# Recurrent retention and a SiLU block on one core: three more units of k and q transposed by the DMA

## The chip, the core and the metric

The kernel runs on one core of a Trainium2 chip. Its engines are TensorE (PE: matrix products; its weight loads are shown apart as PEld), VectorE (DVE), ScalarE (ACT), GpSimd (POOL) and SyncE (SP), which here issues nearly all DMA transfers. The metric is the device time of one execution in microseconds; the number given for the kernel is the median of its runs. All matrix work is in 32-bit floats, split into parts so that products are exact enough.

## The reference

First a recurrent retention over 4 batches (b), 8 heads (h), 768 positions and 64 channels; then a two-layer block with SiLU on the result, with heads and channels side by side as 512 features:

```python
gamma = 1.0 - 2.0 ** (-5.0 - np.arange(H, dtype=np.float32))
for t in range(S):
    state = gamma[None, :, None, None] * state + np.einsum('bhd,bhe->bhde', k[:, :, t], v[:, :, t])
    y[:, :, t] = scale * np.einsum('bhd,bhde->bhe', q[:, :, t], state)
x = y.transpose(0, 2, 1, 3).reshape(B * S, H * D)
h = x @ w_in                      # 3072 x 512 by 512 x 2048
g = h * (1.0 / (1.0 + np.exp(-h)))
return g @ w_out                  # 3072 x 2048 by 2048 x 512
```

## The kernel before

**Units, visits, steps.** The 768 positions are cut into 6 chunks (c) of 128. A unit is one chunk of one batch, numbered 4c + b, so there are 24. Each unit goes through three stages in three successive visits. In visit m, unit m is staged (k and q are transposed, so that channels lie on partitions), unit m-1 gets its score and state products (L452, L462), and unit m-2 its output y (L501), which is split into three parts of x for the first layer. A step (c, f) is the first layer for one chunk and one of 16 slices f of 128 hidden features: eight products into the PSUM tile ha and four into hb (`multiply`, L650), then in `close_steps` a copy of ha by ScalarE (L660), a subtraction of hb by VectorE (L665), and the SiLU by ScalarE (L670). SP stores the result g to DRAM. After the 96 steps the second layer reads g back (L967).

**Order.** TensorE runs in the order of the program text. On the other engines, after the opening part, a planner orders the instructions by priority and by when it thinks their inputs are there; `queue(ins)` only says "not before `ins`". Things that are to follow a step's copy of ha are put into the list `behind_copy`, things that are to follow its subtraction into `behind_next`. The list `steps` fixes the order of steps: after (1,15) come (2,8) to (2,15), then (3,0), (3,1) and so on; (2,3) to (2,7) lie some twenty steps earlier. The list `at` says behind which step a visit stands: visit 14 behind (1,15), 15 behind (2,9), 16 behind (2,11), 17 behind (2,13), so that they are two steps apart; from visit 18 behind (3,1) on they are four steps apart.

**Two ways to transpose.** `stage_t` (L429 to L438) lets TensorE transpose k and q of a unit, four 128 x 128 transposes each into PSUM (L436), and ScalarE copy them out (L438). It is used for units below FAR = 17. From unit 17 on the DMA does it, in 16-bit planes: `part_t` (L407) lets GpSimd separate the high and low halves of the 32-bit words of q and of k (L412); `turn_t` (L416) lets SP issue one transposing DMA for each (L419); `join_t` (L422) lets ScalarE interleave the halves again (L426). For unit m these stand in visit m, one step later, and three steps later. `scale_k` (L382, L398) multiplies k by its decay factors, after the parting and two steps later; `scale_q` (L403) multiplies the joined q by gq, and `next_chunk` (L350) advances gq by a chunk, in four ScalarE instructions.

**Buffers.** Tiles of one tag share a number of buffers. k and the planes of q share "kf" (3), q and its turned planes "qf" (2), the planes of k and the transposed k "kt" (2), the turned k and the transposed q "qt" (3). The tag "wl" (1) holds the low part while a weight slice is split (L123 to L128). The y of chunk 2 are read back from DRAM by `late_y` (L583, batches 0 and 2 into "kt", 1 and 3 into "qt") and split by `late_x` (L557 to L563). g uses three buffers "hs". `load` (L145) issues the loads of k, q, v: in visit m for unit m+2, or m+1 where the unit is above FAR, and always m+1 for v. Between visits VectorE and ScalarE also turn the weights, which arrive as 64-bit words, into 32-bit floats (L196 to L217).

**The fence.** In each visit a GpSimd write of a token (L377) separates two groups of the products of y; a parting in a visit stands behind that fence on GpSimd.

Of the kernel before, what the change touches and what calls it, by code (L numbers as in the profile page):

```python
# [13 lines left out]
FP32 = mybir.dt.float32  # L14
# [19 lines left out]
def kernel(  # L34
# [31 lines left out]
    C = 128  # L66
# [72 lines left out]
    kqv = {"k": {}, "q": {}, "v": {}}  # L139
    EARLY = 2 * B  # L140

    FAR = 4 * B + 1
    early = {}

    def load(name, n):  # L145
        if n >= len(units):
            return
        c, b = units[n]
        src = {"k": k, "q": q, "v": v}[name]
        if n < EARLY:  # L150

            if n not in early:
                early[n] = wpool.tile([128, 3, H, D], FP32, tag=f"w{4 + n}", name=f"kqv_{n}")
            t = early[n][:, "kqv".index(name)]
        else:
            t = ld.tile([128, H, D], FP32, tag=f"{name}f", name=f"{name}f_{n}",
                        bufs=2 if name == "q" else 3)
        nc.sync.dma_start(out=t, in_=src[b, :, ds(c * C, C)].rearrange("h t d -> t h d"))
        kqv[name][n] = t
# [244 lines left out]

    planes, turned = {}, {}

    def part_t(n):  # L407

        for name, (p, tag, bufs) in (("q", (ld, "kf", 3)), ("k", (one, "kt", 2))):
            src = kqv[name].pop(n) if name == "q" else kqv[name][n]  # L410
            t = p.tile([128, 2 * H * D], U16, tag=tag, name=f"{name}p_{n}", bufs=bufs)
            nc.gpsimd.tensor_copy(out=t.rearrange("p (w h d) -> p w h d", w=2, h=H),  # L412
                                  in_=src.bitcast(U16).rearrange("p h (d w) -> p w h d", w=2))
            planes[name, n] = t

    def turn_t(n):  # L416
# [5 lines left out]
    def join_t(name, n):  # L422

        to, bufs = (qt, 3) if name == "q" else (kt, 2)
        to[n] = one.tile([128, HP, C], FP32, tag=f"{name}t", name=f"{name}t_{n}", bufs=bufs)
        nc.scalar.copy(out=to[n].bitcast(U16).rearrange("p a (t w) -> p w a t", w=2),  # L426
                       in_=turned.pop((name, n)).rearrange("p (w a) t -> p w a t", w=2))
# [153 lines left out]
    y_late = {}  # L581

    def late_y(b):  # L583
        tag = ("kt", "qt")[b % 2]
        y_late[b] = one.tile([128, KIN, C], FP32, tag=tag, name=f"yr_{b}", bufs=2 + b % 2)
        nc.sync.dma_start(out=y_late[b], in_=y_dram[b])

    def late_x(b):
# [9 lines left out]
    def halves(m):  # L598

        first, mid, last = (0 <= m - i < len(units) for i in range(3))  # L600
        if first and m < FAR:
            stage_t(m)
        if last:
            scores, states_with, yp = stage_y(m - 2)
            scores()
            states_with(0)
        yield
        if mid:
            sc, sums = score_tile(m - 1)
            stage_s(m - 1, sums)  # L610
            stage_a(m - 1, sc)
            if 1 < m <= 3 * B + 1 and units[m - 1][1] == 0:
                next_chunk()

            with queue(taken_out[0]) if m > 3 * B + 1 else ExitStack():
                finish_a(m - 1, sc, sums)
            scale_q(m - 1)
            if m > 3 * B + 1 and units[m - 1][1] == B - 1:

                behind_copy.append(next_chunk)  # L620
        if first and m < FAR:
            scale_k(m)
        if last:
            states_with(1)
            finish_y(m - 2, yp)

        if FAR <= m < len(units):
            with queue(fenced[0]):
                part_t(m)
        for name in "kqv":  # L630
            for n in (m + 1, m + 2):
                if n >= EARLY and n == (m + 1 if name == "v" or n > FAR else m + 2):
                    load(name, n)
        if EARLY + 2 <= m < 3 * B + 2:
            with queue(masked[0]):
                end_w()
                if m != 3 * B:
                    begin_w()


    pending = []

    def product_in(c, f):
# [264 lines left out]
    for i, x in enumerate(at):  # L908
# [4 lines left out]
    behind[1, NF - 1] = lambda: [late_x(3), visit(EARLY + 6)]  # L913


    far = {steps.index(x): EARLY + 6 + i for i, x in enumerate(at)
           if FAR <= EARLY + 6 + i < len(units)}
    for n, (c, f) in enumerate(steps):
        if n - 2 in far:
            behind_next.append(lambda m=far[n - 2]: scale_k(m))  # L920
        if n - 3 in far:
            behind_copy.append(lambda m=far[n - 3]: [join_t(name, m) for name in "qk"])
        product_in(c, f)
        put_g(1)
        store_w()
        if (c, f) in takes:
            take_w(taken_out[0], n < len(pairs + three))
        behind.get((c, f), lambda: None)()
        if n - 1 in far:
            turn_t(far[n - 1])  # L930
        if c == NC - 1:
            if f == 0:
                for i in range(W_READ):
                    get_w(i)
            if f < NF - 4:
                w_out(f)
            if f >= NF - 6:
                if f == NF - 6:
                    for n in range(G_AHEAD):
                        get(n)  # L940
                if f >= NF - S_AHEAD:
                    split(f - NF + S_AHEAD)
# [84 lines left out]
```

## Time and profile before

| | |
|---|---|
| time, median of 3 runs | 622.0 us (619.96 to 622.71) |
| the profiled execution: time, span | 619.42 us, 617.6 us |
| TensorE clock granted | full |
| span from 97 to 170 us | steps of chunks 0 to 2, visit 14 at the end |
| span from 170 to 204 us | visits 14 to 17, steps (2,8) to (2,15) |
| span from 204 to 303 us | chunks 3 and 4, visits 18 to 25 |
| span from 350 us | second layer |
| TensorE transposes (L436) | 68 for k, 68 for q; 272 and 273 ns each at the median, overlapping |
| planes parted (L412) | 7 for q, 7 for k; 1042 and 1051 ns |
| transposing DMAs (L419) | 7 and 7; issue 1304 and 1282 ns, landing after 4.1 and 3.6 us |
| ScalarE joins (L426) | 7 for q and 7 for k, about 1.36 us each |
| ScalarE evacuations of transposes (L438) | 0.58 us each |

A row of the page or of an answer of the trace gives the line of the kernel, the engine, the operation and the tiles that it writes and reads; "x4" is the number of instructions. In a list in order of time, the first number is the start in the span, the second the duration, and a bracket at the end says how long the engine was idle before and who released it.

### The profile page before, as it was taken

Reading aid. Unit: us, or ns where it says so; the run is one execution under the profiler, and the core shown is the slowest. Engines: PE = TensorE matmul, PEld = TensorE weight load, DVE = VectorE, ACT = ScalarE, POOL = GpSimd, SP = SyncE. Lnnn points to the kernel's source line nnn. Section 1 sums busy time; section 2 is a strip of 40 time slices with the busy share of each in tenths; the row PEclk is TensorE's granted clock in tenths of the full one; section 3 lists DMA queues with packets and bytes.
Section 4 is the critical chain, followed back from the end, with each engine's and each line's share of the span. In section 5 each row is a group of like instructions: output and inputs, shape, how many; then the busy total and the mean of one; then the engine's idle time right before and its main releaser. Section 6 shows DMA issues by size and latency. Waiting matters only on the chain.

```text
span 617.6 us, 13494 instructions
## 1 busy us (share of the span) xinstructions
PE 603.8 (98%) x5384; PEld 497.5 (81%) x5384; DVE 422.9 (68%) x731; ACT 313.0 (51%) x595; POOL 22.6 (4%) x79
## 2 busy tenths in 40 slices
PE   6899999999999999999999999999999999999997
PEld 5777887888888888888788888888888888888886
DVE  4998889899789877676699773635545453654631
ACT  6678896676654667766587732312221221412311
POOL 3000000000001111120000000000000000000000
PEclk9999999999999999999999999999999999999999
DMA  9989896464677999989767542533524433442301
GB/s 191 225 203 228 243 240 200 157 198 157 222 177 208 259 255 239 259 223 282 255 230 248 203 139 68 171 102 100 173 69 134 140 103 102 141 132 89 116 1 68
DMA packets 137999, 107.31 MB, mean 174 GB/s; under 512 B 94801, under 2 KB 103249, under 8 KB 137937
## 3 DMA queue, kind: packets, MB, share of 16 engines
q1 hardware_dynamic: 135056, 101.21, 57.5%
q10 hardware_dynamic: 2880, 5.24, 2.3%
q8 instruction: 42, 0.69, 0.5%
q14 instruction: 21, 0.16, 0.1%
HBM read 66.06 MB, written 36.70 MB: 166 GB/s over the span
## 4 chain that ended last, share of the span: by engine, by line
PE 84%; DVE 0%; DVEq 0%; issue 0%; POOLq 0%
PE ha L650 25%; PE o L967 21%; PE oa L967 14%; PE hb L650 12%; PE ob L967 7%; PE y L501 2%; PE sc L462 1%; PE sc L452 1%; PE o L975 0%; PE oa L975 0%; PE qp L436 0%; PE kp L436 0%; PE ob L975 0%; DVE o L993 0%; DVEq L1022 0%
## 5 line engine op out<-in xcount | busy, mean ns | idle before, releaser
L650 PE MATMUL ha<-xt,wi 128*128 128x512 f32 x768 | 193.8, 394 | 1.3 <-ACT xt L557 0.7
L650 PEld LDWEIGHTS ha<-xt,wi 128*128 128x128 f32 x768 | 141.9, 188 | 33.6 <-ACT wi L126 1.2
L967 PE MATMUL o<-wo,gs 128*128 128x512 f32 x564 | 143.2, 389 | 0.0
L717 DVE TENSOR_TENSOR gs<-gr,gs 128x512 fp32r<-128x512 f32 x96 | 62.1, 685 | 90.3 <-ACT gs L715 90.3
L967 PEld LDWEIGHTS o<-wo,gs 128*128 128x128 f32 x564 | 105.9, 188 | 21.9
L715 ACT ACTIVATE gs<-gr 128x512 fp32r<-128x512 f32 x96 | 53.6, 621 | 134.2 <-issue 131.8
L967 PE MATMUL oa<-wo,gs 128*128 128x512 f32 x376 | 115.8, 389 | 0.0
L650 PE MATMUL hb<-xt,wi 128*128 128x512 f32 x384 | 102.9, 390 | 0.0
L665 DVE TENSOR_TENSOR g<-g,hb 128x512 f32<-128x512 f32 x96 | 65.6, 683 | 42.0 <-ACT g L660 26.3
L650 PEld LDWEIGHTS hb<-xt,wi 128*128 128x128 f32 x384 | 71.8, 188 | 15.5 <-DVE g L665 0.2
L670 ACT ACTIVATE g<-g 128x512 f32<-128x512 f32 x96 | 60.3, 628 | 47.1 <-DVE g L665 47.1
L967 PEld LDWEIGHTS oa<-wo,gs 128*128 128x128 f32 x376 | 70.6, 188 | 14.7
L967 PE MATMUL ob<-wo,gs 128*128 128x512 f32 x188 | 73.7, 392 | 0.0
L660 ACT ACTIVATE g<-ha 128x512 f32<-128x512 f32 x96 | 57.0, 594 | 31.9 <-PE ha L650 15.1
L718 DVE SCALAR_TENSOR_TENSOR gs<-gs 128x512 fp32r<-128x512 f32 x96 | 62.0, 683 | 0.0
L967 PEld LDWEIGHTS ob<-wo,gs 128*128 128x128 f32 x188 | 35.3, 188 | 8.7 <-DVE o L985 1.6
L196 ACT ACTIVATE ca<-wf 128x512 f32<-128x512 f32 x32 | 21.4, 668 | 6.0 <-DVE cw L217 5.5
L212 DVE SCALAR_TENSOR_TENSOR ca<-wf,ca 128x512 f32<-128x512 uint32 x32 | 22.7, 710 | 0.5
L984 ACT ACTIVATE o<-o 128x512 f32<-128x512 f32 x10 | 6.0, 600 | 33.4 <-PE o L967 33.0
L206 DVE SCALAR_TENSOR_TENSOR cs<-ca,cs 128x512 uint32<-128x512 uint32 x32 | 22.1, 691 | 0.9
L501 PE MATMUL y<-qt,mid 64*64 64x64 f32 x384 | 20.2, 224 | 1.0 <-POOL token L377 1.0
L470 DVE TENSOR_TENSOR am<-sc,decay 128x512 f32<-128x512 f32 x24 | 16.5, 687 | 6.6 <-PE sc L462 6.5
(93 smaller groups left out, 562.0 us busy)
## 6 DMA issues: line engine op xcount, KB each, us to landing
gd<-g SPq DMA_DIRECT2D x96, 256.0 KB, 3.1
gr<-gd SPq DMA_DIRECT2D x96, 256.0 KB, 2.7
wf<-in_moe_w_out_dram SPq DMA_DIRECT2D x16, 512.0 KB, 4.2
out_dram<-o ACTq DMA_DIRECT2D x20, 256.0 KB, 2.1
wf<-in_moe_w_in_dram SPq DMA_DIRECT2D x16, 256.0 KB, 4.2
wf<-in_moe_w_in_dram SPq DMA_DIRECT2D x32, 128.0 KB, 4.0
kf<-in_k_dram SPq DMA_DIRECT2D x16, 256.0 KB, 5.1
qf<-in_q_dram SPq DMA_DIRECT2D x16, 256.0 KB, 4.0
```

Of the source, the lines that this page charges most:

```text
L196: nc.scalar.activation(out=a.bitcast(FP32), in_=hi.bitcast(FP32), func=AF.Abs, scale=65536.0)
L206: nc.vector.scalar_tensor_tensor(out=s, in0=a, scalar=3, in1=s, op0=ALU.logical_shift_left, op1=ALU.bitwise_or)
L212: nc.vector.scalar_tensor_tensor(out=p.bitcast(FP32), in0=lo, scalar=2.0 ** -52, in1=p.bitcast(FP32), op0=ALU.mult, op1=ALU.mult)
L501: i = nc.tensor.matmul(yp[ts(e, D), o, a, :], lhsT=lhsT, rhs=rhs, start=(e, o) not in started, stop=True, skip_group_check=True).ins
L650: nc.tensor.matmul(hb if i == 2 else ha, lhsT=w_sb[f][:, i, ts(kk, 128)], rhs=xt[c][:, i, kk, :], start=kk == 0 and i != 1, stop=kk == KIN ...
L660: copied[:] = [nc.scalar.activation(out=hs, in_=ha, func=AF.Copy, scale=ONE_E).ins]
L665: taken_out[:] = [nc.vector.tensor_tensor(out=hs, in0=hs, in1=hb, op=ALU.subtract).ins]
L670: nc.scalar.activation(out=hs, in_=hs, func=AF.Silu)
L715: nc.scalar.activation(out=t[:, 0, :], in_=g, func=AF.Copy, scale=HALF)
L717: nc.vector.tensor_tensor(out=t[:, 1, :], in0=g, in1=high, op=ALU.subtract)
L718: nc.vector.scalar_tensor_tensor(out=t[:, 2, :], in0=t[:, 1, :].bitcast(FP32), scalar=-1.0 / EPS, in1=high, op0=ALU.mult, op1=ALU.add)
L967: nc.tensor.matmul(o, lhsT=g, rhs=wo[f][:, i, :], start=f == 0 and i != 1, stop=f == NF - 1 and i != 0)
```

## The change

FAR goes from 17 to 14, and a second limit, LATER = 18, is added. Units 14 to 17 are now transposed by the DMA on an earlier time table, units 18 to 23 on the one of before. Unit 14 is parted behind the subtraction of step (2,3), turned two steps later, and joined at the step after visit 14. Units 15, 16 and 17 are parted one visit ahead (in visits 14, 15, 16), turned at the step after that visit, and joined at the step after their own visit. `scale_k` for units up to 17 stands in the unit's own visit. Loads: k and q of unit 15 move to step (2,7), q of 16 to step (2,8); k of unit 16 goes into the "wl" buffer. The y of batches 1 and 3 that are read back use "wl" as well, in place of "qt". Joins are put at the head of the list `behind_copy`, so that they stand ahead of the scaling of gq.

```diff
-    FAR = 4 * B + 1
+    FAR = 3 * B + 2
+    LATER = 4 * B + 2
@@ load
+        if n == 4 * B and name == "k":
+            t = conv.tile([128, H, D], FP32, tag="wl", name=f"kf_{n}")
+            nc.sync.dma_start(out=t, in_=src[b, :, ds(c * C, C)].rearrange("h t d -> t h d"))
+            kqv[name][n] = t
+            return
@@ part_t
-    def part_t(n):
+    def part_t(n, after=None):
...
+            if after is not None:
+                tc.add_manual_dep(i, after.name, mybir.DependencyInfo(
+                    mybir.DependencyClass.Sync, mybir.DependencyReason.DATA), reason="later")
@@ late_y
-        tag = ("kt", "qt")[b % 2]
-        y_late[b] = one.tile([128, KIN, C], FP32, tag=tag, name=f"yr_{b}", bufs=2 + b % 2)
+        p, tag, bufs = ((one, "kt", 2), (conv, "wl", 1))[b % 2]
+        y_late[b] = p.tile([128, KIN, C], FP32, tag=tag, name=f"yr_{b}", bufs=bufs)
@@ halves
-        if first and m < FAR:
+        if first and m < LATER:
             scale_k(m)
...
-        if FAR <= m < len(units):
+        n = m if m >= LATER else m + 1
+        if FAR < n < len(units) and (m < LATER - 1 or m >= LATER):
             with queue(fenced[0]):
-                part_t(m)
+                part_t(n)
...
-                if n >= EARLY and n == (m + 1 if name == "v" or n > FAR else m + 2):
+                if (n, name) not in apart and n >= EARLY and n == (
+                        m + 1 if name == "v" or n >= LATER else m + 2):
                     load(name, n)
+    apart = [(FAR + 1, "k"), (FAR + 1, "q"), (FAR + 2, "q")]
@@ the loop over steps
-    far = {steps.index(x): EARLY + 6 + i for i, x in enumerate(at)
-           if FAR <= EARLY + 6 + i < len(units)}
+    far = {m: steps.index(x) for m, x in enumerate(at, EARLY + 6)}
+    first_far = steps.index((2, 3))
+    parts = {first_far: FAR}
+    turns_at = {first_far + 2: FAR}
+    turns_at.update({far[m] + 1: m + 1 for m in range(FAR, LATER - 1)})
+    joins_at = {far[m] + 1: m for m in range(FAR, LATER)}
+    for m in range(LATER, len(units)):
+        turns_at[far[m] + 1], joins_at[far[m] + 3] = m, m
+    scales_at = {far[m] + 2: m for m in range(LATER, len(units))}
+    loads_at = {first_far + 4: [("k", FAR + 1), ("q", FAR + 1)], far[FAR] + 1: [("q", FAR + 2)]}
     for n, (c, f) in enumerate(steps):
-        if n - 2 in far:
-            behind_next.append(lambda m=far[n - 2]: scale_k(m))
-        if n - 3 in far:
-            behind_copy.append(lambda m=far[n - 3]: [join_t(name, m) for name in "qk"])
+        if n in scales_at:
+            behind_next.append(lambda m=scales_at[n]: scale_k(m))
+        if n in joins_at:
+            behind_copy.insert(0, lambda m=joins_at[n]: [join_t(name, m) for name in "qk"])
+        if n in parts:
+            behind_next.append(lambda m=parts[n]: part_t(m, taken_out[0]))
         product_in(c, f)
...
-        if n - 1 in far:
-            turn_t(far[n - 1])
+        if n in turns_at:
+            turn_t(turns_at[n])
+        for name, m in loads_at.get(n, ()):
+            load(name, m)
```

More of the change, by code (lines that the diff above doesn't have):

```diff
@@ L411, in part_t @@
             t = p.tile([128, 2 * H * D], U16, tag=tag, name=f"{name}p_{n}", bufs=bufs)
-            nc.gpsimd.tensor_copy(out=t.rearrange("p (w h d) -> p w h d", w=2, h=H),
-                                  in_=src.bitcast(U16).rearrange("p h (d w) -> p w h d", w=2))
+            i = nc.gpsimd.tensor_copy(
+                out=t.rearrange("p (w h d) -> p w h d", w=2, h=H),
+                in_=src.bitcast(U16).rearrange("p h (d w) -> p w h d", w=2)).ins
+            if after is not None:
+                tc.add_manual_dep(i, after.name, mybir.DependencyInfo(
+                    mybir.DependencyClass.Sync, mybir.DependencyReason.DATA), reason="later")
             planes[name, n] = t
```

## The prediction

> **What bounds the kernel now.** I read the page first, then the chain of waits, then the busy times by stretch, then the order of instructions on VectorE, GpSimd, ScalarE and the DMA queue between 97 and 215 us, where units 14 to 17 are handled.
>
> ```profile
> PE 603.8 (98%) x5384; PEld 497.5 (81%) x5384; DVE 422.9 (68%) x731; ACT 313.0 (51%) x595; POOL 22.6 (4%) x79
> ...
> PE 84%; DVE 0%; DVEq 0%; issue 0%; POOLq 0%
> ```
>
> TensorE works for 603.8 of 617.6 us and is the only engine of weight in the chain that ended last. A TensorE instruction that goes is time won, as long as no new gap takes its place.
>
> ```profile
> 97.00:170.00 73.00, 72.61 (x320) 60.06 (x321) 63.16 (x111) 47.94 (x85) 0.00 (x0) 1.00 0.56 182
> 170.00:204.00 34.00, 34.00 (x636) 28.84 (x635) 30.75 (x56) 19.16 (x36) 3.05 (x6) 1.00 0.74 202
> 204.00:303.00 99.00, 98.70 (x1257) 81.61 (x1256) 71.82 (x125) 64.48 (x100) 13.37 (x20) 1.00 0.94 256
> ```
>
> These are stretches: length, then busy us of PE, PEld, DVE, ACT, POOL, then clock, DMA share, GB/s. In 170:204, where the four visits of units 14 to 17 stand only two steps apart, TensorE has no gap at all, but VectorE is 90% busy (30.75 of 34), against 73% after 204 us, where visits stand four steps apart. So the change takes TensorE work out of the one stretch where the next engine has least room.
>
> ```profile
> 169.86 0.46 PE hb L650 x2
> 170.32 0.44 PE kp L436 x4
> 170.76 0.44 PE qp L436 x4
> 171.19 0.86 PE y L501 x48
> 172.05 0.47 PE sc L452 x32
> 172.52 0.47 PE sc L462 x32
> 172.99 0.23 PE y L501 x16
> 173.22 2.04 PE ha L650 x8
> ```
>
> This is the chain in visit 14. The two rows of L436 are the transposes that the change removes: 0.88 us.
>
> ```profile
> 196.60 0.68 DVE L665 TENSOR_TENSOR g<-g,hb 128x512 f32<-128x512 f32 x1
> 197.19 0.42 DVE L209 TENSOR_SCALAR ca<-cs 128x512 uint32<-128x512 uint32 x1
> 197.65 1.41 DVE L212 SCALAR_TENSOR_TENSOR ca<-wf,ca 128x512 f32<-128x512 uint32 x1
> 199.09 1.41 DVE L217 TENSOR_TENSOR cw<-cs,ca 128x512 f32<-128x512 f32 x1
> 200.42 0.68 DVE L470 TENSOR_TENSOR am<-sc,decay 128x512 f32<-128x512 f32 x1
> ```
>
> ```profile
> 197.26 1.25 POOL L412 COPY qp<-qf 128x1024 uint16<-128x1024 uint16 x1
> 198.45 1.50 POOL L412 COPY kp<-kf 128x1024 uint16<-128x1024 uint16 x1
> ```
>
> Here the parting of unit 17 (POOL) meets VectorE: L212 and L217, 0.69 us each elsewhere, take 1.41, and the copies take 1.25 and 1.50 where the least is 1.04 and 1.05.
>
> [...] L212 and L217 lost 0.72 us each, while the PSUM-reading L470 beside later partings kept 0.69. [...] A two-step round (178.6 to 187.2) moves eight pieces of 256 KB (k, q, v, two stores of g, a 512 KB weight, its store) for 0.83 x 8.6 = 7.1 us of all 16 engines; 187.2 to 195.8 gives 0.76 x 8.6 = 6.5; so 6.8, or 0.85 a piece. A four-step round with transposes (222 to 235) takes 1.04 x 6 + 0.84 x 7 = 12.1 us for ten pieces (8.5) and two transposes. My estimate is 3.6 us for a unit's two transposes.
>
> **The change part by part**, against the profiled execution (span 617.6, its time 619.42; the three runs have median 622.0, from 619.96 to 622.71, so the profiled one is the fastest of four and 2.6 below the median; gains are carried over to the median).
>
> 1. *TensorE.* From one post-visit product to the next with transposes: 173.22 to 181.78 = 8.56 us. Without (visit 17): 190.35 to 198.04 = 7.69. So 0.87 a visit, three visits (14, 15, 16): **2.6 us gone**. PSUM turns: the transposes of k took a turn of the three h banks; without it each ha waits for the subtraction (L665) of two steps before, as it does now after visit 17.
>
> 2. *Parting on POOL.* Six more copies of about 1.05, 6.3 us on an engine with 4% busy. That alone is free. Unit 14's pair sits behind the subtraction of step (2,3), at 116.31 to 117.00; VectorE then waits 1.73 us for hb, so its 2.1 us are almost covered; without that cover it costs at most 1.4 as in visit 17, and VectorE has room there. The pairs of 15, 16 and 17 move to visits 14, 15, 16, and visit 17 loses its pair (1.44 us of VectorE returned). VectorE's price for each: below 0.24 us (L403 took 0.92 instead of 0.68 beside a later pair), above 1.44 (visit 17), or 2.1 if both copies block in full (visit 14[...]). [...] I take 0.8 on average, 2.4 in all; ends 0.7 and 4.3.
>
> 3. *VectorE against the shorter round.* Its round from one visit to the next was 182.32 to 190.89 = 8.57, of which 0.56 was waiting for ScalarE's copy of ha: 8.0 us of work in a round that becomes 7.69. It falls behind by 0.3 a round before any lock. What ends the stretch is the bank of step (2,14): ha of (3,0), now at 203.55, needs L665 of (2,14), now 202.28 to about 202.9. Ideal new start: 203.55 - 2.6 = 200.9. New L665: that of (2,8) can start 1.25 earlier than now (176.26 had 1.25 of idle ahead, waiting for the copy of ha), so about 175.0; three rounds of 8.0 bring it to 199.0; plus 2.4 for locks 201.4, done 202.0. **Stall 1.1 us.** With 0.7: 199.7, done 200.3, no stall. With 4.3: done 203.9, stall 3.0. Right behind it the last parts of x (L560, L563) of unit 15 are due about as late, with less than 1 us more room.
>
> 4. *ScalarE.* Six evacuations of 0.58 go, six joins (L426) of 1.36 come: +1.56 a unit. Round 178.6 to 187.2 goes from 4.58 busy to 6.1 of 7.69, the next one, with the four scalings of gq (1.27), from 5.68 to 7.2. The joins follow a copy of ha; behind them wait the Silu of the same step and the copy of the next ha: copy 0.5, joins 2.5, Silu 0.55 make 3.6 us before the next copy, while VectorE wants that copy after some 3.2 from the L665 ahead. So VectorE waits a further 0.4 or so in some rounds; TensorE also needs the joins before L462 of the visit. Bounds: 0 (order and slack hide it) and 1.5. I take 0.3. Putting the joins ahead of gq is worth up to 1.27 us once, at (2,12), where TensorE's L462 would otherwise have about 0.4 us of room; it wins nothing against the kernel before, which had no joins there.
>
> 5. *SP and DMA.* Six more transposes at 1.3 us of issue each; behind them on SP wait a load of q or k and the stores of g, and the next copy into a g buffer (three) waits for a store three steps old. Each transposes' buffer is free only after the join before it (turn of 15 behind the join of 14: about 176 and 177.4). DMA: 171 to 209 holds 0.73 x 31 + 1.05 x 7 = 30 us of work including unit 17's; two more units make 37 in a stretch of 38 - 2.6 = 35.4. That is full; the stretch after it runs at 0.94 without a TensorE gap of note (0.3 us in 99). Transposes land in 3.1 to 5.7 us; between turn and join lies a round of 7.69 less the wait for the buffer, so the room is 1 to 3 us. Bounds: 0 and 6.5 (rival C). I take 0.
>
> 6. *Loads and y.* The moved loads of k and q of 15 and 16 wait on SP for buffers only briefly: k of 16 takes the "wl" tile after L560 of late_x(3), now done at 171.9, and lands in 4 to 5 us against a parting due at 179. y of batch 3 waits in the same tile for late_x(1) (L560 done 164.15, against issue at 163.9 now): under 0.5 us, hidden, as it is read only at 170.5. If the tile were not free, SP would hold the stores of g: that is in rival D.
>
> Sum: -2.6 + 1.1 + 0.3 = **-1.2 us**: 618.2 for the profiled execution, and 622.0 - 1.2 = 620.8 for the median.
>
> **The rivals.** *A: full gain.* VectorE's locks cost little or the planner sets its instructions where POOL is idle: -2.0 to -2.6, about 619.6. For it: the later partings cost 0.24 each. Against: the one parting in a two-step round cost 1.44. *B: VectorE eats it all.* Locks of 4.3 us: stall 3.0 and 0.3 on top, +0.7: 622.7. For it: 8.0 us of work in 7.69. Against: visit 14's lock falls partly into the 1.25 us of idle. *C: slower.* The joins come late: DMA full, so transposes of units 15, 16, 17 land about 2 us after their join stands at the head of ScalarE; all behind it (Silu, copy of ha, subtraction, bank) waits, and TensorE stops 2.2 us in each of three rounds: 6.6 - 2.6 = +4.0: 626.0. It decides once a landing takes over 7 us (the longest now 5.7). For it: a 105% full DMA. Against: a share of 1.05 at 202 to 209 already gave 4.6 and 3.8. *D: the change doesn't do what it says*, because the planner gives the shared tiles (kt, wl) in another order and a parting or a y waits long for one; it would cost a late x for step (2,8), 2 to 4 us: net +1, 623.
>
> **How the numbers follow.** Forecast (-0.5 to -1.9): 0.40, its own range 620.1 to 621.5. A: 0.25. B: 0.17. C: 0.12. D: 0.06. A change of 0.5% (3.1 us) is about what a measurement here can tell from none; the limits are 618.9 and 625.1. No case reaches 618.9 by itself; the four executions spread 3.3 us, so I give about a third of A and of the forecast to it: 0.22. Slower: C and a little of B and D, 0.15. Same: 0.63. The range from 617.6 (A with the spread) to 624.4 (B and D with it) leaves out most of C.
>
> **What would show it.** Rows L436 fall by 24 transposes; L412, L419, L426 rise by 6 each. Rounds from visit 14 to visit 17 of 7.69 would prove step 1; a gap of about 1 us ahead of ha of (3,0), released by L665 or L560, step 3; L212, L217, L398 or L403 of 0.9 to 1.4 us beside a POOL copy, step 2; no ScalarE wait on qw or kw over 1 us, step 5. I am wrong if the first gap comes at L462 on a join, if no gap comes at all, or if the stretch before 170 us changes.

## The result, and the profile after

The changed kernel is slower: its median is 627.0 us (15 runs, 624.11 to 630.82), that of the kernel before in the same session 623.33 us (15 runs, 619.57 to 625.67). The ratio of the runs is 1.0067 (it isn't the quotient of the two medians), with a 95% interval of [1.0046, 1.0088]: slower by less than 1%, but clear of noise. The forecast was 620.8 us with a range up to 624.4, so it missed on the slow side. Of the 6.2 us between forecast and median, 1.3 lie in the kernel before itself, whose median over 15 runs is above the 622.0 us of three runs that the forecast started from.

The profiled execution of the changed kernel has a time of 627.0 us and a span of 624.9 us, 7.3 us more than the span before. First its page: busy times, then the chain that ended last.

```profile
PE 604.9 (97%) x5360; PEld 498.0 (80%) x5360; DVE 424.2 (68%) x731; ACT 316.9 (51%) x595; POOL 29.0 (5%) x85
...
PE 77%; DVE 3%; DMA 2%; issue 1%; ACT 1%; POOL 0%; SPq 0%; DVEq 0%; POOLq 0%; ACTq 0%
```

The edits did what they say: 24 TensorE instructions fewer, six GpSimd copies more. But the chain, which before was TensorE with almost nothing beside it, now runs through VectorE and the DMA for 5% of the span. Next, the busy times by stretch (length, then busy us of PE, PEld, DVE, ACT, POOL, then clock, DMA share, GB/s).

```profile
17.00:37.00 20.00, 17.46 (x387) 14.75 (x389) 15.26 (x29) 11.28 (x24) 0.26 (x3) 0.74 0.93 213
170.00:204.00 34.00, 29.14 (x545) 23.61 (x548) 27.50 (x47) 21.72 (x33) 7.43 (x9) 1.00 0.96 226
204.00:303.00 99.00, 99.00 (x1266) 81.99 (x1258) 72.87 (x128) 63.77 (x98) 13.33 (x20) 1.00 0.95 251
```

Two things are to be seen. In 170:204 TensorE idles for 4.9 of 34 us where it had no gap before, and the DMA share has gone from 0.74 to 0.96. And in 17:37 the clock granted is 0.74; that is in the opening part, whose text is untouched, and it put everything behind it 4.2 us later in this execution (the last product of step (1,15) ends at 174.5 instead of 170.3). To keep the second out of the comparison I measure one stretch by its own ends: from the end of step (1,15) to the first product behind visit 18. I call it the stretch. It was 40.78 us, it became 43.70 us, so **2.9 us of loss lie in it**. The two parts behind it (to the first product behind visit 25, then to the second layer) are unchanged: 91.48 and 49.20 before, 91.47 and 49.18 after.

Who made TensorE wait in 170 to 206 us is said by the view of waits (us in total, times, longest):

```profile
PE y L511 <- DVE xt L570: 4.8, 3, 3.7
...
DVE kf L404 <- POOL kp L418: 3.4, 1, 3.4
```

All of TensorE's idle time has one releaser: L570 (L560 before), the VectorE instruction that forms the second part of x and is the last to read y. It has to be done before the products of y of the next visit may write that PSUM tile. The three gaps stand ahead of visits 15, 16 and 17 in TensorE's order of instructions (start, duration; the bracket is the idle time and who ended it):

```profile
182.45 0.69 PE L511 MATMUL y<-am,vf 64*64 64x64 f32 x32 [0.23 <-DVE xt L570]
...
191.46 0.69 PE L511 MATMUL y<-am,vf 64*64 64x64 f32 x32 [0.87 <-DVE xt L570]
...
202.96 0.69 PE L511 MATMUL y<-am,vf 64*64 64x64 f32 x32 [3.72 <-DVE xt L570]
```

From the first product of y in one visit to that in the next, visits 14 to 18 are now 7.99, 9.01, 11.50 and 13.25 us apart, where they were 8.57, 8.57, 7.69 and 13.13 (the transposes that went stood ahead of y in visits 14, 15 and 16, so the first two distances hold 0.87 us of the gain each and the rest lies ahead of visit 14). Against the gain of 2.6 us stand 4.8 us of gaps (-2.6 + 4.8 = +2.2); the other 0.7 us of the 2.9 are late starts and longer products of under 0.5 us each.

Why L570 is late ahead of visit 17 is told by VectorE's order of instructions:

```profile
195.00 0.69 DVE L223 TENSOR_TENSOR cw<-cs,ca 128x512 f32<-128x512 f32 x1
199.06 0.69 DVE L404 TENSOR_TENSOR kf<-kf,gk 128x512 f32<-128x512 f32 x1 [3.37 <-POOL kp L418]
199.67 0.68 DVE L480 TENSOR_TENSOR am<-sc,decay 128x512 f32<-128x512 f32 x1
...
201.53 0.68 DVE L678 TENSOR_TENSOR g<-g,hb 128x512 f32<-128x512 f32 x1
202.13 0.68 DVE L570 TENSOR_TENSOR xt<-y,xt 128x512 fp32r<-128x512 f32 x1
```

VectorE stands still for 3.37 us in front of L404, the scaling of the k of unit 17, and everything behind it stands too, up to L570: between L223 at 195.00 us and L404 at 199.06 no instruction starts on VectorE. L404 multiplies k in place, so it has to wait until GpSimd has copied the planes out. GpSimd's order of instructions:

```profile
185.24 1.14 POOL L418 COPY kp<-kf 128x1024 uint16<-128x1024 uint16 x1
192.54 0.09 POOL L383 MEMSET token<- 1x1 f32 x1 [6.16 <-PE y L511]
197.00 1.04 POOL L418 COPY qp<-qf 128x1024 uint16<-128x1024 uint16 x1 [4.37 <-DMA qw<-qp]
197.98 1.05 POOL L418 COPY kp<-kf 128x1024 uint16<-128x1024 uint16 x1
```

The fence (L383) was open at 192.6, but the parting of unit 17 waits 4.37 us more for a plane buffer, which the transposing DMA of the unit before still reads. The chain of waits shows what lies behind that (start, us, what; "issue" pieces and others are left out where the dots are):

```profile
185.52 1.42 DVE ca L218
...
186.96 0.70 DVE cw L223
...
187.68 0.04 ACT ca L202
...
188.26 0.58 ACT xt L567
188.84 0.49 ACT g L673
189.33 1.25 ACT qt L436
190.58 0.21 ACT kt L436
190.79 0.83 issue
191.62 0.16 ACT g L683
191.78 5.10 DMA qw<-qp
...
197.00 0.73 POOL qp L418
197.73 0.24 issue
197.98 1.06 POOL kp L418
199.04 0.02 issue
199.06 0.69 DVE kf L404
```

The DMA queue's own order shows why that transpose went out so late:

```profile
189.52 2.17 SPq L689 DMA_DIRECT2D gd<-g  x1
191.78 1.30 SPq L429 DMA_TRANSPOSE qw<-qp  x1
```

Unit 16 had been parted by 186.4, but its transpose stood on SP behind a store of g, which waited for a SiLU (L683), which on ScalarE stood behind the joins of unit 15 (L436). The joins were late in their turn: in front of them ScalarE had stood idle for 2.12 us before L202, the first instruction of a weight conversion, until VectorE had finished the conversion before (L223, 187.65 us). VectorE had had no idle time of over 0.1 us since 175.1 us. So one chain runs through five queues and two visits: a conversion on VectorE, joins of 15 and SiLU on ScalarE, store and turn of 16 on SP, parting of 17 on GpSimd, scaling of 17 on VectorE, y on TensorE. The parts of the sum that I priced (VectorE beside GpSimd copies, VectorE's round, joins, transposes) are links of it; the link that carries the wait to TensorE, the scaling moved into the visit, I had not priced at all.

### The profile page after: what moved, and what is told of

It is laid out like the page before. It is cut to its first block, busy times and chain, and to the rows that moved or that the text cites. A ratio compares the mean times of both kernels' runs of the same rounds, so it can differ in the third digit from the quotient of the medians.

```text
span 624.9 us, 13463 instructions
## 1 busy us (share of the span) xinstructions
PE 604.9 (97%) x5360; PEld 498.0 (80%) x5360; DVE 424.2 (68%) x731; ACT 316.9 (51%) x595; POOL 29.0 (5%) x85
## 4 chain that ended last, share of the span: by engine, by line
PE 77%; DVE 3%; DMA 2%; issue 1%; ACT 1%; POOL 0%; SPq 0%; DVEq 0%; POOLq 0%; ACTq 0%
PE ha L663 22%; PE o L992 20%; PE oa L992 14%; PE hb L663 11%; PE ob L992 7%; PE y L511 2%; DMA gd<-g 1%; DMA qw<-qp 1%; PE sc L472 1%; PE sc L462 1%; DVE xt L570 1%; PE o L1000 0%; DVE g L678 0%; DVE kf L404 0%; DVE xt L573 0%
## 5 line engine op out<-in xcount | busy, mean ns | idle before, releaser
L683 ACT ACTIVATE g<-g 128x512 f32<-128x512 f32 x96 | 60.3, 628 | 50.7 <-DVE g L678 50.6
L202 ACT ACTIVATE ca<-wf 128x512 f32<-128x512 f32 x32 | 21.4, 668 | 5.5 <-DVE cw L223 4.2
L218 DVE SCALAR_TENSOR_TENSOR ca<-wf,ca 128x512 f32<-128x512 uint32 x32 | 22.7, 709 | 0.5
L212 DVE SCALAR_TENSOR_TENSOR cs<-ca,cs 128x512 uint32<-128x512 uint32 x32 | 22.1, 689 | 0.8
```

What stands on the lines that cost most here:

```text
L202: nc.scalar.activation(out=a.bitcast(FP32), in_=hi.bitcast(FP32), func=AF.Abs, scale=65536.0)
L212: nc.vector.scalar_tensor_tensor(out=s, in0=a, scalar=3, in1=s, op0=ALU.logical_shift_left, op1=ALU.bitwise_or)
L218: nc.vector.scalar_tensor_tensor(out=p.bitcast(FP32), in0=lo, scalar=2.0 ** -52, in1=p.bitcast(FP32), op0=ALU.mult, op1=ALU.mult)
L683: nc.scalar.activation(out=hs, in_=hs, func=AF.Silu)
```

## The experiments

All twelve kernels are compared with the kernel before in the same session; the diffs are against the changed kernel unless said otherwise. "Stretch" is the one defined above, and "then" the part up to visit 25; both are from the profiled execution. Changed kernel: 43.70 and 91.47. In the stretches of e2, e7 and e10 TensorE's clock was at half for a while, which is up to 1.7, 2.4 and 1.7 us of them (last section).

| run | ratio, 95% interval | stretch, then (us) | TensorE's waits in the stretch |
|---|---|---|---|
| e1 | 1.0059 [1.0037, 1.0082] | 44.37, 91.84 | 3.6 for ScalarE's copy of ha, 0.9 for L570 |
| e2 | 1.0104 [1.0077, 1.0130] | 44.98, 95.09 | 4.2 for L570, 0.6 for the copy |
| e3 | 1.0047 [1.0030, 1.0064] | 40.45, 94.47 | 0.9 for L570, 0.4 for the copy, 0.3 for L573 |
| e4 | 1.0002 [0.9987, 1.0017] | 41.09, 91.47 | 1.0 for a join |
| e5 | 1.0034 [1.0020, 1.0048] | 40.78, 91.47 | 1.9 for L570 |
| e6 | 0.9999 [0.9979, 1.0020] | 40.56, 91.47 | 1.3 for L570, 0.2 for the copy |
| e7 | 1.0051 [1.0020, 1.0082] | 44.75, 91.56 | 4.0 for L570 |
| e8 | 1.0018 [1.0002, 1.0035] | 39.12, 91.48 | 0.4 for the copy, 0.2 for L570 |
| e9 | 1.0002 [0.9976, 1.0027] | 40.24, 91.77 | 1.2 for the copy, 0.2 for L570 |
| e10 | 1.0057 [1.0038, 1.0076] | 44.44, 91.47 | 3.2 for the copy, 0.2 for L570 |
| e11 | 0.9982 [0.9967, 0.9996] | 40.27, 92.13 | none |
| e12 | 0.9999 [0.9982, 1.0017] | 40.67, 91.47 | 0.7 for a join, 0.2 each for the copy and L570 |

### e1: the scaling of unit 17 back to where it was

```diff
-        if first and m < LATER:
+        if first and m < LATER - 1:
             scale_k(m)
...
-    scales_at = {far[m] + 2: m for m in range(LATER, len(units))}
+    scales_at = {far[m] + 2: m for m in range(LATER - 1, len(units))}
```

> One edit to the changed kernel: k of unit 17 is scaled behind the subtraction two steps after visit 17, as in the kernel before, and no longer inside visit 17. Theory 1 (the wait of the scaling for the parting of unit 17 holds VectorE in order, 3.4 us, and through the output bank of y TensorE for 3.7 us): the gap ahead of visit 17 falls from 3.7 us to under 1, VectorE no longer waits for GpSimd there, and the time falls by about 3 us against the changed kernel, to a ratio of 1.001 to 1.003 to the kernel before. Theory 2 ([...] the wait for GpSimd only fills time it would lose anyway): the gap stays above 2.5 us, ratio 1.005 or more. Theory 3 (DMA is full, joins are late): as theory 2, and ScalarE waits for turned planes.

Measured: ratio 1.0059, which can't be told from the changed kernel's 1.0067, so the 3 us expected of theory 1 did not come. The gap of 3.72 us ahead of visit 17 is gone (theory 2, VectorE late by its own work, had it stay above 2.5), that of 0.9 ahead of visit 16 stays, and two new ones come. TensorE's waits between 168 and 215 us:

```profile
PE hb L663 <- ACT g L673: 3.6, 2, 2.3
PE y L511 <- DVE xt L570: 0.9, 1, 0.9
```

And ScalarE's order of instructions around the second one:

```profile
208.47 0.64 ACT L683 ACTIVATE g<-g 128x512 f32<-128x512 f32 x1 [0.75 <-DVE g L678]
212.50 0.60 ACT L673 ACTIVATE g<-ha 128x512 f32<-128x512 f32 x1 [3.39 <-DMA gd<-g]
```

The copy of ha waits 3.39 us for a buffer of g that a store has not yet left; until the copy is done, its PSUM bank isn't free for the next product. So it is shown that the wait of the scaling makes the first gap, and that taking it away doesn't pay: behind it a second limit stands at nearly the same place in time, late stores of g. Over the whole execution ScalarE waits 13.4 us for them, where it waits 6.1 us in the changed kernel and 4.5 in the kernel before.

### e2 and e3: weight conversions moved out of the stretch

VectorE's six instructions that convert a weight slice (L205 to L223) follow the steps in the list `takes`. Two of the three that stand in the stretch are moved, alone (e2) and together with e1's edit (e3).

```diff
-    takes += [(0, NF - 2), (2, half), (2, half + 2), (2, half + 4)]
-    takes += [(3, f) for f in (0, 3, 7, 11, 14)]
+    takes += [(0, NF - 2), (1, NF - 3), (2, half)]
+    takes += [(3, f) for f in (0, 3, 5, 7, 11, 14)]
```

> One edit to the changed kernel: two of the weight conversions (3.3 us of VectorE each) leave the stretch of the two-step visits, from steps (2,10) and (2,12) to (1,13) and (3,5). Theory 1: the gaps of 0.2 and 0.9 us ahead of visits 15 and 16 go (the output bank is drained in time), but the parting of unit 17 still waits for the buffer of unit 16's planes, so a gap of 1 to 3 us ahead of visit 17 stays; ratio 1.000 to 1.004. Theory 2: with 6.6 us less of VectorE work in the stretch all three gaps go, ratio 0.996 to 0.997. Theory 3: the gap ahead of visit 17 stays at 3 us or more, ratio 1.005.

> Both edits, that of e1_scale17_late and that of e2_takes_moved, on the changed kernel. Theories 1 and 2: no gap of over 0.3 us in front of visits 15, 16 and 17, so the 2.6 us of removed transposes are won: ratio 0.995 to 0.998. Theory 3 (DMA): gaps at the score products, released by joins, ratio 1.000 or more.

Measured: e2 is 1.0104 (6 runs), the slowest of all. The gap ahead of visit 17 is still 3.11 us: with less work right in front of L404, VectorE only stands longer at it (5.0 us instead of 3.4), so it isn't that work that makes L570 late. But e2 leaves the conversion of step (2,8) in its place, and that is the one at the head of the chain above: in e2 too ScalarE waits 2.6 us at L202 for its end, ahead of the joins of unit 15. So VectorE's load one visit earlier stays a possible root, and no run takes that conversion away. e3 missed its forecast of 0.995 to 0.998. Its stretch falls to 40.45 us, 3.9 less than in e1, but the part behind it grows by 3.0 us (91.47 to 94.47). There TensorE waits 1.0 us for a copy of ha and 1.0 us for joins, the two waits that late transfers make; the conversion moved there brings its loads and stores into a part whose DMA share was 0.95 already. That these cause the waits is argued, not shown by itself.

### e4: unit 14 alone

Units 15 and 16 go back to TensorE, unit 17 to the table of before; only unit 14 takes the new way.

```diff
-    LATER = 4 * B + 2
+    LATER = 4 * B + 1
...
-        if first and m < FAR:
+        if first and m < LATER and m != FAR:
             stage_t(m)
...
-    turns_at.update({far[m] + 1: m + 1 for m in range(FAR, LATER - 1)})
-    joins_at = {far[m] + 1: m for m in range(FAR, LATER)}
+    joins_at = {far[FAR] + 1: FAR}
```

> Of the change only unit 14 is kept (parted behind step (2,3), turned at (2,5), joined at (2,8)), with the y of batches 1 and 3 in the tile of the split; units 15 and 16 are transposed by TensorE, unit 17 and later on the old time table. Theories 1 and 2: visit 14 is 0.87 us shorter and no gap comes, ratio 0.998 to 0.9995. Theory 3, or a loss before visit 14 (the first 170 us): no gain or a loss, ratio 1.001 or more.

Measured: 1.0002, between the two forecasts: no loss and no gain. Visit 14 is 0.87 us shorter, and 1.0 us comes back at the scores of visit 18, which wait for the join of unit 17. ScalarE's order of instructions there:

```profile
207.09 0.60 ACT L667 ACTIVATE g<-ha 128x512 f32<-128x512 f32 x1 [0.68 <-DMA gd<-g]
209.56 1.37 ACT L431 COPY qt<-qw 128x1024 uint16<-128x1024 uint16 x1 [1.87 <-DMA qw<-qp]
```

So the gain of one visit is real, and the loss of the whole change belongs to units 15 to 17.

### e5: fewer conversions in the stretch, none added behind it

e1's edit, one conversion ahead of the stretch, one in the last chunk.

```diff
-    takes += [(0, NF - 2), (2, half), (2, half + 2), (2, half + 4)]
+    takes += [(0, NF - 2), (1, NF - 3), (2, half)]
...
-    takes += [(5, f) for f in (2, 5, 8)]
+    takes += [(5, f) for f in (0, 2, 5, 8)]
```

> As e1_scale17_late, and two weight conversions leave the stretch of the two-step visits for steps with room: (2,10) becomes (1,13), (2,12) is dropped and one at (5,0) added, so that none is added between visits 18 and 25 (where e3_both got new gaps of 2.1 us). Theory 1+2 (VectorE): from the end of (1,15) to the first product of visit 18 the time falls from 41.9 us in the changed kernel to under 37.5 (36.3 without any gap; 38.9 before), ratio 0.996 to 0.998. Theory 3 (the DMA engines are full, and stores of g or turned planes land late): 38 to 40 us, with ScalarE waiting for stores of g; ratio 0.999 to 1.003.

Measured (the 41.9 and 38.9 us of the text above end at visit 18, some 2 us before the end of the stretch): 1.0034 [1.0020, 1.0048], lower than e1, though the two intervals overlap. The stretch is 40.78 us, what it was before the change, with 1.9 us of waiting for L570 left in it; 1.0 us more is lost behind visit 25 (50.19 instead of 49.18).

### e6: e1 with less for the DMA to do

The v of units 15 to 17 and the weight slices 19 to 21 are not loaded; the v of unit 14 and slice 18 stand in for them. All instructions of the other engines stay.

```diff
+        if name == "v" and 14 < n < 18:
+            kqv[name][n] = kqv[name][n - 1]
+            return
...
+        if 18 < i < 22:
+            staged[i] = staged[i - 1]
+            return
```

> As e1_scale17_late, with transfers left out: v of units 15 to 17 is not loaded (v of unit 14 is used), and the weight slices 19 to 21 are not loaded (slice 18 is used); 3 x 256 KB and 3 x 512 KB less in or about the stretch, some 7.7 us of all DMA engines by 0.85 us for 256 KB. The other instructions of the engines stay. Theory 3: the waits of ScalarE's copy of ha for stores of g (6.0 us in e1_scale17_late) fall under 1.5 us and the two gaps of 1.3 and 2.4 us at the products go; the time falls by 2.5 us or more against e1_scale17_late. Theory 2 (VectorE and ScalarE alone): the gaps stay, within 1 us of e1_scale17_late.

Measured: 0.9999 [0.9979, 1.0020] against e1's 1.0059. TensorE's waits between 168 and 215 us:

```profile
PE y L517 <- DVE xt L576: 1.3, 3, 0.9
PE hb L669 <- ACT g L679: 0.2, 1, 0.2
```

The 3.6 us that TensorE waited for the copies in e1 have become 0.2, and ScalarE's own waits for stores of g fell from 6.0 to 1.2 us. This shows that transfers are the second limit. It doesn't separate the 16 DMA engines from SP's queue, since the loads left out free both.

### e7: the stores of g from another queue

e1's edit, and the stores of steps (2,8) to (3,1) are issued by ScalarE.

```diff
-            nc.sync.dma_start(out=g_dram[c, f], in_=g)
+            on = nc.scalar if c == 2 and f > 7 or c == 3 and f < 2 else nc.sync
+            on.dma_start(out=g_dram[c, f], in_=g)
```

> As e1_scale17_late, with the stores of g of steps (2,8) to (3,1) issued by ScalarE's queue in place of SP's, so that they don't stand behind transposes and loads there that wait for buffers. If SP's order is what makes the stores late: the waits of ScalarE for stores of g fall under 1.5 us and the gaps at the products go, 2.5 us less than e1_scale17_late. If the DMA engines are full (theory 3): landing still takes up to 6 to 8 us, the waits stay above 3 us, and the time is within 1 us of e1_scale17_late or worse.

Measured: 1.0051 [1.0020, 1.0082], no better. The waits for the copies are gone (ScalarE waits 1.2 us for stores of g instead of e1's 6.0). That doesn't prove SP's order guilty, as the changed kernel, with its gap of 3.7 us, has no such waits of TensorE either, with all stores on SP: a gap ahead gives the stores time. And e7 has a gap of that size, because now the first mechanism closes one visit earlier, at unit 16, with the k planes instead of the q planes. VectorE's order of instructions, then GpSimd's:

```profile
182.77 0.69 DVE L223 TENSOR_TENSOR cw<-cs,ca 128x512 f32<-128x512 f32 x1
186.23 0.69 DVE L404 TENSOR_TENSOR kf<-kf,gk 128x512 f32<-128x512 f32 x1 [2.77 <-POOL kp L418]
```

```profile
180.69 1.04 POOL L418 COPY qp<-qf 128x1024 uint16<-128x1024 uint16 x1 [1.09 <-DMA qf<-in_q_dram]
185.16 1.04 POOL L418 COPY kp<-kf 128x1024 uint16<-128x1024 uint16 x1 [3.42 <-DMA kw<-kp]
```

That k transpose was issued as early as in the changed kernel (7.2 us behind step (1,15) in both), but took 7.4 us to land (issued at 177.75, the copy that waits for it starts at 185.16) instead of 3.4. So with the stores off SP's queue the planes still aren't turned in time; here the transfer itself is slow, not its place in the queue. A miss as a remedy, it shows the wait at L404 in a second place. It also showed something of the clock, told at the end.

### e8, e9 and e10: y drained first

L570 and L573 of a unit of chunk 3 were held back together until the subtraction of the next step; now L570 isn't held, L573 is. e8 is e5 with this edit; e9 keeps one conversion more in the stretch and none in the last chunk; e10 is e1 with this edit alone.

```diff
+        if c == NC // 2 and b < B - 0:
+            lower()
+            behind_next.append(third)
+            return
```

> As e5_takes_out, and the subtraction that drains the output bank of y in visits 14 to 17 is no longer held back behind the next step's subtraction of hb. Theory 1+2: the gap of 0.9 us ahead of visit 16 (released by that subtraction in e1, e2 and e3) falls to under 0.3 us, 0.6 us less than e5_takes_out. If the bank is not what holds TensorE, the gap stays, or comes back at the next product.

> As e8_drain_first, but only one weight conversion leaves the stretch ((2,10) becomes (1,13)); (2,12) stays and none is added at (5,0), where e8_drain_first lost 1.4 us. Both theories (VectorE's order, then the DMA): from the end of (1,15) to the first product behind visit 18 between 39.0 and 40.3 us (40.8 before, 38.2 without a gap), nothing lost after visit 25, ratio 0.997 to 1.001. If VectorE's 3.3 us more in the stretch bring back gaps ahead of visits 16 and 17 of over 1 us in sum: 1.002 or more.

> The changed kernel with two edits of VectorE's order alone: k of unit 17 is scaled two steps later, and the subtraction that drains the output bank of y in visits 14 to 17 is not held back. If the order on VectorE is the whole loss: no gaps but those of its 8.0 us of work in rounds of 7.7 us, stretch 38.2 to 39.5, ratio 0.996 to 0.999. If the DMA is the second limit: the gaps at the products released by the copy of ha (3.6 us in e1_scale17_late) stay above 2 us, stretch 41 to 43, ratio 1.002 to 1.005.

Measured: in all three the wait for L570 falls to 0.2 us, and visits 14 and 15 are 7.69 us apart, where it was 8.57: there the gain of 0.87 us is seen whole. From visit 15 to 16 it still takes 8.5 to 8.6. e8 has the shortest stretch of all, 39.12 us, 1.7 less than before, but pays 1.4 us behind visit 25 for the conversion moved there, and its ratio is 1.0018 [1.0002, 1.0035]. e9 is 1.0002. And e10, where VectorE's order is mended and nothing else, is still 1.0057: TensorE's waits between 168 and 215 us

```profile
PE hb L667 <- ACT g L677: 3.2, 2, 2.8
PE y L511 <- DVE xt L570: 0.2, 1, 0.2
```

are those for the copies of ha again. So the late transfers alone are enough for the loss. Whether VectorE's order alone would be isn't shown: both runs that leave transfers out, e6 and e12, also take the scaling of unit 17 out of the visit.

### e12: both limits lifted

e10 with the transfers of e6 left out (the v of units 15 to 17, slices 19 to 21).

> As e10_order_only, with the transfers of e6_less_dma left out (v of units 15 to 17: v of unit 14 is used; weight slices 19 to 21: slice 18 is used). If VectorE's order and the DMA together are the whole loss, the stretch is within 1 us of the 38.2 without a gap and the ratio 0.995 to 0.997. If a third limit is there (ScalarE's joins, locks), gaps of over 1.5 us stay and the ratio is 0.998 or more.

Measured: 0.9999 [0.9982, 1.0017]; the gain that I expected of it did not come. The rounds are 7.69, 8.45 and 7.78 us, but from visit 17 to visit 18 it takes 14.80 instead of 13.13, and the stretch is 40.67 us, no better than e6's 40.56. Something else holds TensorE there; of its marked waits the longest is for a join:

```profile
PE sc L478 <- ACT kt L442: 0.7, 1, 0.7
PE hb L673 <- ACT g L683: 0.2, 1, 0.2
PE y L517 <- DVE xt L576: 0.2, 1, 0.2
```

These 1.1 us are less than the 2.5 us by which the stretch stands above its full gain (40.78 - 2.6 = 38.2); where the other 1.4 lie is not settled.

### e11: a smaller change

e4 with one edit more: unit 17 is parted in visit 16, turned at (2,12) and joined at (2,14), so that its join comes early enough for visit 18. Its scaling stays where it was before the change.

```diff
-        n = m if m >= LATER else m + 1
-        if FAR < n < len(units) and (m < LATER - 1 or m >= LATER):
+        n = m + 1 if m == LATER - 1 else m
+        if LATER <= n < len(units) and m != LATER:
...
+    del turns_at[far[LATER] + 1], joins_at[far[LATER] + 3]
+    turns_at[far[LATER - 1] + 1], joins_at[far[LATER] + 1] = LATER, LATER
```

> As e4_unit14_alone (15 and 16 by TensorE), and unit 17 on the table of the change (parted in visit 16, turned at (2,12), joined at (2,14)), its scaling two steps behind visit 17. In e4_unit14_alone TensorE waited 0.95 us in visit 18 for the late join of unit 17. If that wait took the gain: it goes, the stretch is 39.9 (one visit of 0.87 us less), ratio 0.998 to 0.9995. If the gain was lost elsewhere (opening, clock): ratio 1.000 or more with the same stretch.

Measured: 621.18 us (22 runs) against 622.44 (51), ratio 0.9982 [0.9967, 0.9996]. It has the lowest ratio here and is faster than the changed kernel beyond doubt. That it beats the kernel before rests on an interval that ends 0.04% below 1, the only one of twelve that does, and its profile doesn't show a gain: the stretch is 0.5 us shorter and the part behind it 0.65 us longer (0.4 us of it a wait for a join). Its runs also had a higher mean clock, 0.9976 against 0.9958 for the kernel before; by the line worked out below that is about 0.6 of the 1.26 us between the medians, an estimate. In the stretch TensorE has no gap again:

```profile
170.00:204.00 34.00, 34.00 (x632) 28.66 (x631) 31.22 (x57) 21.61 (x37) 3.20 (x6) 1.00 0.79 197
```

With one unit more by the DMA and one moved forward, at the two ends of the stretch, instead of three more units in a row, the DMA share is 0.79 instead of 0.96.

## Why the prediction was wrong

Two terms of the sum failed. The scaling of k moved into the visit had no term at all, and brought a wait of 3.37 us that TensorE felt as 3.72. The DMA and SP were taken as 0, and cost 3.6 us where that wait is gone (e1). The other parts follow in their order.

**Part 1 (TensorE, -0.87 us a visit): right.** It is seen whole between visits 14 and 15 of e8, e9 and e10 (7.69 where the round was 8.57), and in visit 14 of e4. From visit 15 to 16 no run shows it whole; other waits cover it.

**Part 2 (what the sum calls locks, 2.4 us): right as a price, wrong in where it is paid.** All that the traces show under this name is that some VectorE instructions take longer while a GpSimd copy runs (before: L212 and L217, 1.41 us instead of 0.69); why, they don't show. The instructions that did so in the profile after were L573 (1.41 us instead of 0.69), L404 (1.52 for 0.68), L218 (1.41 for 0.69) and L215 (0.67 for 0.42): 2.5 us. Two of them:

```profile
176.40 1.41 DVE L573 SCALAR_TENSOR_TENSOR xt<-xt 128x512 fp32r<-128x512 f32 x1
177.73 1.52 DVE L404 TENSOR_TENSOR kf<-kf,gk 128x512 f32<-128x512 f32 x1
```

All four lie between 176.4 and 186.9 us, in the run of VectorE without idle time that ends with L223, so they delay the head of the chain and not a bank of h. Up to 2.1 us of it, ScalarE's wait at L202, could go with them; that is an estimate, and no run tests it.

What failed in this part is what it leaves out. It takes "six more copies" as free for GpSimd itself and prices only what they cost VectorE; it doesn't ask what the copies wait for, nor that `scale_k` moved into the visit waits for them in order. That wait was 3.37 us (e1 takes it away, e7 shows it at the neighbouring unit). It stood in the diff: the condition on `scale_k` changed from FAR to LATER, and I did not ask what is queued behind the wait that this adds.

**Part 3 (VectorE against the shorter round, stall 1.1 us): the engine was right, the place wrong.** I wrote that "what ends the stretch is the bank of step (2,14)" and mentioned the last parts of x in half a sentence, as due about as late. TensorE never waited for that bank in the stretch; it waited 4.8 us for L570, three times, once in each round. y has one PSUM tile and is written again after two steps, so its drain is due in every round, not at the end. The two shorter gaps (0.23 and 0.87 us) fit VectorE's fall behind, as L570 drawn forward takes them down to 0.2 us or less in e8 to e10; the 3.72 us go through the scaling, as e1 shows, though VectorE's full round stands at the head of that chain too. The first gap stood at y, which was none of the signs of being wrong that I had named.

**Part 4 (joins, 0.3 us): not seen in the changed kernel as a wait of its own,** but the joins are a link of the chain, since the SiLU and the store behind them hold SP. In e4 (1.0 us) and e12 (0.7 us) TensorE does wait for a join.

**Part 5 (SP and DMA, taken as 0): wrong, and the largest error by itself.** The sum that I made, 37 us of DMA work in 35.4, said full; I took 0 because the stretch behind ran at 0.94 without a gap. The sum was about right: share times length gives about 31 us of DMA work in the stretch before (0.77 of 40.78) and 40 after (0.91 of 43.70). e1 and e10 show 3.6 and 3.2 us of TensorE's time lost to late stores, and e6, with other transfers left out, shows them gone. How much of it is SP's order and how much the 16 DMA engines, e6 and e7 don't tell. The bounds of 0 and 6.5 us held it.

**Rival C** had the resource and about the time (626.0), with a chance of 0.12. Its place was not where TensorE first stopped: not a late join at the head of ScalarE, but a late transposing DMA that keeps a plane buffer from GpSimd, and behind that a late store that keeps a g buffer from ScalarE. That a wait for a plane buffer brings the 3.37 us is read from the trace; a fourth buffer would test it by itself, and wasn't tried. What made the transpose late in the first place, VectorE's round or the DMA, stays open.

**The sum.** The 2.9 us of the stretch are part of the difference of the medians, 3.7 us. The rest fits the clock: the 15 runs of the changed kernel have a mean clock of 0.9930, while the kernel before had 0.9958 to 0.9972 in the three sessions of the experiments, and a straight line through the 15 runs rises by 3.5 us for each 0.01 less. That is 1.0 to 1.5 us, an estimate. The last section has what is known of it.

## What to carry to other kernels

When an instruction is moved, list what it waits for in its new place and everything that is queued behind it on its engine; here one scaling, moved by two steps, tied TensorE to a DMA of the unit before. Look for every tile that has one buffer and is written in each round: its last reader is due in each round. And where a change trades work of the bound engine for transfers in a stretch where the DMA sum comes out above the length, take that sum at its word, and try the change with the traded units far apart before trying them in a row.

## What the runs showed of the hardware

**TensorE's clock fell to half at three gaps of some 3 us, and not at a fourth.** In e7 TensorE's gap of 3.75 us runs from 186.38 to 190.13 us. The clock falls at 188.15, inside the gap, and stays at half for 6.8 us, as stretches of 2 us show (the number behind the five engines is the clock):

```profile
188.00:190.00 2.00, 0.00 (x0) 0.00 (x0) 2.00 (x5) 0.58 (x2) 0.00 (x0) 0.54 1.24 158
190.00:192.00 2.00, 1.87 (x69) 1.90 (x73) 1.97 (x5) 0.53 (x2) 0.12 (x2) 0.50 1.05 192
...
194.00:196.00 2.00, 2.00 (x7) 1.62 (x8) 1.97 (x4) 0.51 (x1) 0.92 (x1) 0.76 0.85 273
```

In e2 it falls at the end of the gap of 3.11 us and stays at half for 3.4 us (0.80, 0.50 and 0.85 in the stretches of 2 us from 200 to 206 us). In e10 it falls 1.3 us after the gap of 2.81 us (0.73 and 0.50 from 208 to 212 us); there eight products of ha take 3.41 us instead of 1.98 and the four of hb behind them 1.30 instead of 1.07, which makes about 3.3 us at half. With the 3.72 us of the changed kernel's profiled execution it stays at 1.00. What decides whether and when the clock falls is not shown by these traces. In e2, e7 and e10 the gap thus cost more than itself; as an estimate from the lengths above, 3.3 or 3.4 us at half are up to 1.7 us of work (e2, e10), and in e7, where 4.8 of the 6.8 us lie behind the gap, up to 2.4. It fits that of the 45 runs of the four kernels with a single gap of 2.3 us or more in this stretch (the changed one, e1, e2, e10) none has a mean clock of 0.999 or above, while 50 of 154 runs of the kernel before have; e7 has 2 of 9. But e3 and e5, without such a gap, have only 7 of 44. That the gaps cause the lower clock in every such run is not shown; in the changed kernel's profiled execution the clock was also at half in the opening part, from 23.6 to 33.9 us.

**Stores of g landed later where the DMA share was higher, transposes only in part.** The transpose of the chain above took 5.1 us from issue to landing, with a DMA share of 1.33 over that time; the median for q in the kernel before is 4.1. In e7 the one for k took 7.4 us, with a share of 1.21 from 180 to 184 us and 1.04 from 184 to 186; the median for k in the kernel before is 3.6. The share alone doesn't settle it: in the changed kernel the transposes for k issued at 123.8 and 181.8 us took 3.1 and 3.4 us at shares of 1.06 and 1.01. The stores of g took, at the median, in the kernel before 2.5 us from 100 to 160 us at a share of 0.55 (23 stores), 4.0 from 204 to 303 us at 0.94 (32 stores). In the changed kernel it was 2.6 from 104 to 164 us at 0.69 (23 stores), and 4.3 from 170 to 206 us at 0.97 (8 stores).
